# All loads of v on SyncE, and the last rows' products with v behind the odd slot's MLP pieces

## The chip, the cores and the metric

The kernel runs on one core of a Trainium2 chip. The metric is device time in microseconds (us) of one execution, the median of several. Engines are named as in the profile: PE (TensorE matmul), PEld (its weight loads), DVE (VectorE), ACT (ScalarE), POOL (GpSimd), SP (SyncE, which here only issues DMAs). A trailing q (SPq, ACTq) is an engine's sequencer: the row is a DMA issue or a wait, not work of the engine.

## The reference

Attention with a top-32 selection, then an MLP with exact GELU, all in fp32:

```python
scores = scale * np.matmul(q, k.transpose(0, 1, 3, 2))      # (8, 8, 576, 576), head_dim 64
kth = np.partition(scores, -top_k, axis=-1)[..., -top_k:-top_k + 1]
scores = np.where(scores >= kth, scores, -1000000000.0)
...
attn_out = np.matmul(attn, v)                               # softmax of what is left, times v
x = np.ascontiguousarray(attn_out.transpose(0, 2, 1, 3)).reshape(B * S, H * D)   # (4608, 512)
h = x @ w_in                                                # (4608, 2048)
g = 0.5 * h * (1.0 + erf(h * inv_sqrt2))
return (g @ w_out).astype(np.float32)
```

## The kernel before

**Items and slots.** Heads are worked in pairs (4 pairs for each of 8 batches). An item is 128 score rows of a pair: `t` = 0 to 3 are full tiles of 128 rows, and the 64 rows that are left over (`t == NM`, "last rows") are put together from two pairs into one item. There are 144 items, 18 for each batch. Even batches have their two last-row items at the end, odd batches at the start, so four last-row items come in a row: 16 to 19, 52 to 55, 88 to 91 and 124 to 127. The loop over `n` (L1174) is the order of the work, written out by hand. Slot `n` issues the scores of item `n + 2`, the top-32 search of item `n` on DVE (`top_k`, L472), the softmax of item `n - 1` on ACT, the transposition of item `n - 2`, the product with v of item `n - 3` (`attend`, L708), and a number of MLP pieces between them (`mlp`, L1093), each a few matmuls. A slot takes about 10 us.

**Transposing through DRAM.** The product with v needs the softmax matrix transposed (tile `pt`). For a "squared" item (L571) this goes by way of memory: `square_p` (L587) turns 32x32 blocks on DVE (L591), `write_p` (L593) issues four DMAs into a DRAM tile `turned` (L601), and a slot later `read_p` (L603) issues four DMAs that read it back into `pt` (L611). Two items share one `pt` tile, of which there is one, so `read_p` of an even item also waits until the products of the pair of items before it are through. All of these are issued by SP.

**Delayed items.** The last-row items of the three later groups (52 to 55, 88 to 91, 124 to 127) are squared and "delayed" (L577): their products with v (L738, 40 matmuls of 64 columns for an item, 20 for each pair of heads) come a slot later than usual. In the first of the groups: item 52 in slot 56 (L1201), item 53 in slot 57, items 54 and 55 together in slot 59. The list `mid` (L1177) is what is left to do in the odd slots: [53] in slot 57 and [54, 55] in slot 59. Ahead of the MLP pieces of the odd slot (`ODD`, two pieces, then one more, L1242 to L1244) the kernel calls `attend` for the items of `mid`, then the copy to `xT` (`copy_x`, L748 on ACT), then `read_p(n - 3)`. I call the three groups group 1, 2 and 3.

**Loads of v.** There are four buffers of v, one for each pair of a batch. When a buffer has been used for the last time, `attend` issues the load of the next batch's v into it (L753 to L755; `load`, L111): for each of two heads a main part (L134, 128 KB) and a tail of 64 rows (L138, 16 KB). For delayed items the mains go to SP and the tails to ACT's queue: 8 loads for item 52 in slot 56, 8 for item 53 in slot 57, and the same in the other groups, 24 tails in all. In slots whose item `n - 2` is squared, `issue` (L99) holds the loads until `write_p` has been issued (`flush`, L106), so the order on SP at a group is: read of 53, write of 54, loads of v after item 52, read of 54, write of 55, loads of v after item 53, two stores of y, read of 55, write of 56, read of 56. Item 56 is a full tile; its read shares a `pt` tile with item 57, and the product that needs both is L727 in slot 60.

**DMA semaphores.** The DMAs issued by SP and by ACT share eight completion semaphores, given out in turn in the order in which the framework schedules the program. Before a DMA is issued, its queue waits until the DMA that had the same semaphore before it has landed. A DMA on SP can so wait for one that ACT issues.

**PSUM.** The products `o`, the transpositions' `tp_t` and the MLP's product `seven` take turns in one bank (`bank`, L274, tag "z" when `few` is set): each has to wait until ACT has copied out what was there before.

Of the kernel before, what the change touches and what calls it, by code (L numbers as in the profile page):

```python
# [14 lines left out]
def kernel(  # L15
# [19 lines left out]
    nc = tc.nc  # L35
# [10 lines left out]
    NP = H // 2  # L46
# [52 lines left out]
    def issue(f):  # L99

        if held[0]:
            late_issues.append(f)
        else:
            f()
# [472 lines left out]
    def delayed(i):  # L577

        return squared(i) and items[i][1] == NM
# [23 lines left out]
    def read_p(i):  # L603

        if squared(i):
            d = turned.pop(i)
            if i % 2 == 0:
                pt_now[0] = pt_tile()
            cols = slice(i % 2 * P, (i % 2 + 1) * P)
            for k in range(P // SQ):  # L610
                nc.sync.dma_start(  # L611
                    out=pt_now[0][k * SQ : (k + 1) * SQ, :, cols], in_=d[:, :, k, :]
                )
# [77 lines left out]
    def copy_x():  # L691
        while copies:
            copies.pop()()
# [12 lines left out]
    def attend(i):  # L706

        if i < 0 or i >= N:  # L708
            return False
        pair, t = items[i]  # L710
        b, at = divmod(pair, NP)
        if t < NM and t % 2 == 0:
            return False
        pt = pt_now[0]
        both = delayed(i) and i - 1 in starts
        o = shared.pop() if both else bank("o")
        off = 2 * TL if both else 0
        n, row = (2 * P, (t - 1) * P) if t < NM else (TL, SM)
        tok = place_of(b, row)
        gap = RING if t == NM else COLS if tok % RING >= COLS else RING - COLS  # L720
        assert read[0] >= tok - gap + n
        c = slice(column(tok), column(tok) + n)
        if t < NM:
            vt = raw_of("v", pair)
            for j in range(NJ):
                for e in range(2):
                    nc.tensor.matmul(  # L727
                        o[e * D : (e + 1) * D, 0:n], lhsT=vt[:, j, e, :],
                        rhs=pt[:, e * NJ + j if j < NM else NM, :],
                        start=(j == 0), stop=(j == NJ - 1),  # L730
                    )
            copies.append(lambda: nc.scalar.copy(out=xT[:, at, c], in_=o[:, 0:n]))
        else:
            for r in range(2):
                vt = raw_of("v", pair + r)
                for j in range(NJ):
                    for e in range(2):
                        nc.tensor.matmul(  # L738
                            o[e * D : (e + 1) * D, off + r * TL : off + (r + 1) * TL],
                            lhsT=vt[:, j, e, :],  # L740
                            rhs=pt[:, e * NJ + j if j < NM else NM, i % 2 * P :][:, half(r, e)],
                            start=(j == 0), stop=(j == NJ - 1),
                        )
            if delayed(i) and i in starts:
                shared.append(o)
            else:
                first = 0 if both else at
                copies.append(lambda: nc.scalar.copy(  # L748
                    out=xT[:, first : at + 2, c],
                    in_=o[:, 0 : off + 2 * TL].rearrange("p (r n) -> p r n", n=TL),  # L750
                ))

        if t == (NM if b % 2 == 0 else NM - 1):  # L753
            for r in range(2 if t == NM else 1):
                issue(lambda r=r: load("v", pair + r + NP, None, nc.scalar if delayed(i) else None))  # L755
        if at == (NP - 1 if t < NM else NP - 2):
            assert n_tok[0] == tok
            n_tok[0] = tok + n
        return True
# [414 lines left out]
    for n in range(ahead):  # L1174

        held[0] = n < N and squared(n - 2)
        mid = [i for i in (n - 5, n - 4) if delayed(i) and n % 2 and (i % 2 or i in starts)]  # L1177
        if not mid:
            read_p(n - 3)
        left[0] = room_in(n)  # L1180
        few[0] = n > START + 2
        eager[0] = n > N
        left[0] += closes(n - 3) - closes(n - 2)
        if not waits(unit_in(n)):
            weights_add(unit_in(n))
        if n > 0:
            larger(n + 1)
        for piece in squares_in.pop(n, []):
            piece()
        if n == 1:  # L1190

            for e in range(2):
                select(0, e)
            for e in range(2):
                softmax(0, e)
        two = few[0] and n % 2 == 0 and n + 3 < N and items[n + 3][1] < NM
        scores(n + 2, two)
        if two:
            scores(n + 3)
        if delayed(n - 4) and n % 2 == 0 and n - 4 not in starts:  # L1200
            product = attend(n - 4)  # L1201
        else:
            product = not delayed(n - 3) and attend(n - 3)
        late = n > START
        if n != 1 and n < START:

            for e in range(2):
                select(n - 1, e)
            softmax(n - 1, 0)
        copy_x()  # L1210
        if n == START:

            for e in range(2):
                select(n - 1, e)
            softmax(n - 1, 0)
        if waits(unit_in(n)):
            weights_size(unit_in(n))
            weights_add(unit_in(n))
        mlp(1)
        if closes(n - 3):  # L1220
            ready[0] = n_tok[0]
        if few[0] and n % 2:
            run_gelus()
        tr = transposes(n - 2)
        if product and n > START and done[0] < len(pieces) and pieces[done[0]][0] > ready[0]:

            for piece in tr[:1]:
                piece(n + 2 if few[0] else None)
            tr, ready[0] = tr[1:], n_tok[0]
        if not few[0] and n > START:  # L1230
            softmax(n - 1, 0)
        mlp(1)
        if n != 1 and not late:
            softmax(n - 1, 1)
        if few[0]:
            softmax(n - 1, 0)
            if mid:
                for i in mid:
                    attend(i)
                copy_x()  # L1240
                read_p(n - 3)
            if n % 2:  # L1242
                mlp(ODD)
        mlp(1)  # L1244
        prep = prep_in.pop(n, [])
        if n == 0:
            weights_size(unit_in(1))
            keep_busy(14, ident)
        if n == START + 1:

            for piece in prep:
                piece(None)
            prep = []
        if len(prep) > 1 and len(tr) == 3:
            tr, prep = tr[:1] + prep[:1] + tr[1:], prep[1:]
        now = tr[:-1]
        if few[0]:
            now, tr, prep = tr + prep[:1], [], prep[1:]
        for x, piece in enumerate(now):
            piece(n + 2 if few[0] else None)  # L1260
            ready[0] = n_tok[0]
            if few[0] and x == 2:
                break
            mlp(1)
        ready[0] = n_tok[0]
        if late:
            softmax(n - 1, 1)
        if n > 0:
            smaller(n + 1)
        add_small(n - 1)  # L1270
        for piece in tr[-1:] + prep:
            piece(None)
            mlp(1)
        if n < START:

            keep_busy(4 if n == 0 else 8 if product else 14 if n < 5 else 18, ident)

        run_gelus()
        mlp(left[0])
        run_gelus()  # L1280
        if n < N:
            top_k(n, lambda: inverse(n - 1), lambda: square_p(n - 2))
            write_p(n - 2)
            flush()
            if n == 0:
                larger(1)
        else:
            inverse(n - 1)
        threshold(n)
        if n == 0:  # L1290
            smaller(1)
        normalise(n - 1)
        sum_up(n + 2)
        if n in sums_in:
            weight_sums(sums_in[n])
        run_small(6)

        if n > 0 and not waits(unit_in(n + 1)):
            weights_size(unit_in(n + 1))
        run_stores()  # L1300
        if n == N:
            run_stores()
        for m in (n + 1, n + 2):

            if m > 2 and waits(unit_in(m)) == (m == n + 1):
                load_weights(m)
        if n < NP:
            load("v", n)
        if n == 5:
            nc.vector.memset(flat["k"][0][TL:, 0:TL], 0.0)  # L1310
            load("q", SQUARES)
            load("k", SQUARES)
# [38 lines left out]
```

## Time and profile before

| | |
|---|---|
| median of 3 runs | 1493.97 us (1492.85 to 1494.8) |
| the profiled execution: its own time | 1493.65 us |
| its span, first to last instruction | 1491.8 us |
| busy: PE, PEld, DVE, ACT, POOL | 1455.1, 1138.3, 1307.8, 1082.4, 1141.1 us |
| mean granted PE clock | 0.994 |
| DMA packets under 512 bytes | 466464 of 544713 |

A line of a timeline has the start, the time from the start to the end of the last of xN like instructions, engine, source line, operation and tiles; in brackets stands the idle time of the engine just before it and what ended it. A line of the waits has who waited for whom, the total in us, how many times, and the longest. Lines of a source view have durations in ns as least/median/most.

### The profile page before, as it was taken

Reading aid. Unit: us, or ns where it says so; the run is one execution under the profiler, and the core shown is the slowest. Engines: PE = TensorE matmul, PEld = TensorE weight load, DVE = VectorE, ACT = ScalarE, POOL = GpSimd, SP = SyncE. Lnnn points to the kernel's source line nnn. Section 1 sums busy time; section 2 is a strip of 40 time slices with the busy share of each in tenths; the row PEclk is TensorE's granted clock in tenths of the full one; section 3 lists DMA queues with packets and bytes.
Section 4 is the critical chain, followed back from the end, with each engine's and each line's share of the span. In section 5 each row is a group of like instructions: output and inputs, shape, how many; then the busy total and the mean of one; then the engine's idle time right before and its main releaser. Section 6 shows DMA issues by size and latency. Waiting matters only on the chain. (4 is left out here: it accounts for less than half of the span.)

```text
span 1491.8 us, 26509 instructions
## 1 busy us (share of the span) xinstructions
PE 1455.1 (98%) x8693; PEld 1138.3 (76%) x8693; DVE 1307.8 (88%) x3331; ACT 1082.4 (73%) x1899; POOL 1141.1 (76%) x1290
## 2 busy tenths in 40 slices
PE   8999999999999998999999998999999999899999
PEld 6776677887777776877777776787777777687787
DVE  7999899999999997999999999799999999798701
ACT  7999877777777775777777776577777777577630
POOL 6877567877888887877898889687788878787732
PEclk9999999999999999999999999999999999999999
DMA  7425210054444355345534347244543524533300
GB/s 198 141 85 132 74 47 1 23 104 96 88 87 88 59 105 121 64 101 107 101 79 88 70 82 148 57 94 95 100 98 73 102 49 93 121 62 74 71 15 15
DMA packets 544713, 127.04 MB, mean 85 GB/s; under 512 B 466464, under 2 KB 536128, under 8 KB 544576
## 3 DMA queue, kind: packets, MB, share of 16 engines
q1 hardware_dynamic: 541392, 124.54, 39.3%
q8 instruction: 69, 1.13, 0.3%
q10 hardware_dynamic: 3120, 0.79, 0.2%
q14 instruction: 68, 0.56, 0.1%
q0 software_dynamic: 64, 0.03, 0.0%
HBM read 80.47 MB, written 44.83 MB: 84 GB/s over the span
## 5 line engine op out<-in xcount | busy, mean ns | idle before, releaser
L790 PE MATMUL h_ps<-xT,w_in_sb 128*128 128x256 f32 (+1 forms) x2560 | 533.6, 361 | 0.0
L790 PEld LDWEIGHTS h_ps<-xT,w_in_sb 128*128 128x128 f32 x2560 | 437.5, 190 | 74.1 <-issue 25.2
L498 DVE MAX8 top<-lists 128x8 f32<-128x576 f32 (+1 forms) x792 | 475.9, 641 | 0.0
L501 DVE MATCH_REPLACE8 lists<-top,lists 128x288 f32<-128x288 f32 (+1 forms) x528 | 307.9, 589 | 0.0
L567 POOL TENSOR_TENSOR s<-s,stat 128x1152 f32<-128x1152 f32 x135 | 285.8, 2117 | 0.3 <-DVE stat L519 0.3
L532 ACT ACTIVATE s<-s,stat 128x576 f32<-128x576 f32 x288 | 225.0, 790 | 13.0 <-POOL stat L512 12.9
L544 ACT ACTIVATE s<-s,stat 128x576 f32<-128x576 f32 x288 | 225.0, 785 | 11.3 <-POOL lists L462 0.7
L525 POOL TENSOR_SCALAR stat<-stat 128x2 f32<-128x2 f32 x144 | 31.3, 218 | 225.3 <-ACT s L544 211.1
L470 POOL TENSOR_TENSOR lists<-lists 128x576 int32<-128x576 int32 x132 | 186.2, 1411 | 4.0
L462 POOL TENSOR_TENSOR lists<-s 128x576 int32<-128x576 int32 x133 | 187.7, 1412 | 0.0
L806 ACT ACTIVATE g<-h_ps 128x512 f32<-128x512 f32 x144 | 78.2, 594 | 106.0 <-PE h_ps L790 105.7
L727 PE MATMUL o<-pt,raw_v 128*64 128x256 f32 x1280 | 152.9, 384 | 1.9 <-ACT s L544 1.3
L727 PEld LDWEIGHTS o<-pt,raw_v 128*64 128x64 f32 x1280 | 86.8, 136 | 86.7 <-issue 43.2
L946 PE MATMUL y_ps<-w_out_sb,sum 128*128 128x256 f32 x472 | 140.4, 379 | 0.0
L410 ACT ACTIVATE s<-s_ps 128x1024 f32<-128x1024 f32 x127 | 125.3, 1034 | 13.9 <-PE s_ps L402 13.8
L402 PE MATMUL s_ps<-kt,qm 64*128 64x512 f32 x512 | 129.4, 618 | 0.8 <-ACT s L408 0.8
L519 DVE RECIPROCAL stat<-stat 128x2 f32<-128x2 f32 x144 | 23.0, 160 | 109.3 <-POOL stat L525 108.7
L946 PE MATMUL y_ps<-w_out_sb,g 128*128 128x256 f32 x480 | 117.2, 388 | 0.0
L672 ACT COPY pt<-tp 128x1024 f32<-128x1024 f32 x73 | 74.4, 1019 | 56.4 <-PE tp L657 56.3
L501 DVE MATCH_REPLACE8 lists<-first,lists 128x288 f32<-128x288 f32 x264 | 114.3, 439 | 0.0
L498 DVE MAX8 first<-lists 128x8 f32<-128x288 f32 x268 | 106.6, 436 | 0.0
L946 PEld LDWEIGHTS y_ps<-w_out_sb,g 128*128 128x128 f32 x480 | 92.8, 195 | 13.3
(162 smaller groups left out, 2499.7 us busy)
## 6 DMA issues: line engine op xcount, KB each, us to landing
turned<-s SPq DMA_DIRECT2D x240, 144.0 KB, 3.6
pt<-turned SPq DMA_DIRECT2D x240, 144.0 KB, 3.2
raw_v<-in_v_dram SPq DMA_DIRECT2D x64, 128.0 KB, 2.7
raw_q<-in_q_dram SPq DMA_DIRECT2D x112, 72.0 KB, 2.4
raw_k<-in_k_dram SPq DMA_DIRECT2D x112, 72.0 KB, 2.4
out_dram<-y SPq DMA_DIRECT2D x30, 256.0 KB, 2.4
w_out_sb<-in_moe_w_in_dram SPq DMA_DIRECT2D x14, 511.8 KB, 4.8
w_out_sb<-in_moe_w_out_dram SPq DMA_DIRECT2D x10, 511.8 KB, 4.0
```

The source lines that it names most:

```text
L402: nc.tensor.matmul(s_ps[:, e], lhsT=q_t[rows, :], rhs=kt[rows, main_keys(pair)], start=True, stop=True)
L410: nc.scalar.activation(spread(s, S + TL, SM), s_ps, func=AF.Copy, scale=scale)
L462: nc.gpsimd.tensor_tensor(t[:, :, 1].bitcast(i32), a.bitcast(i32), b.bitcast(i32), op=ALU.add)
L470: nc.gpsimd.tensor_tensor(into_of(i)[:, :, 1].bitcast(i32), both, top, op=ALU.subtract)
L498: nc.vector.max(x[:, e], src[:, e])
L501: nc.vector.match_replace(dst[:, e], x[:, e], src[:, e], LOWEST)
L532: nc.scalar.activation(s, s, func=AF.Prelu, bias=st["neg"][:, e : e + 1], scale=1.0, alpha=STEEP)
L544: nc.scalar.activation(s, s, func=AF.Exp, bias=st["bias"][:, e : e + 1], scale=1.0, accum_out=st["den"][:, e : e + 1],)
L567: nc.gpsimd.tensor_tensor(s, s, wide, op=ALU.mult)
L727: nc.tensor.matmul(o[e * D : (e + 1) * D, 0:n], lhsT=vt[:, j, e, :], rhs=pt[:, e * NJ + j if j < NM else NM, :], start=(j == 0), stop=(j = ...
L790: nc.tensor.matmul(h_tile(u)[:, i, :], lhsT=w_in_sb[:, ko, f * P : (f + 1) * P], rhs=xT[:, ko, c0 : c0 + n], start=(ko == 0), stop=(ko == ...
L946: nc.tensor.matmul(acc[names][:, k], lhsT=lhsT, rhs=rhs, start=(j == 0 and k == 0), stop=(j == FT // 2 - 1 and k == 1),)
```

## The change

All loads of v after delayed items are issued by SP, the tails too. In odd slots with two items in `mid` (slots 59, 95 and 131), the `ODD` MLP pieces and one more come ahead of the two items' products, of the copy to `xT` and of the read of item `n - 3`; with one item in `mid` (slots 57, 93 and 129) the order stays.

```diff
@@ -752,7 +752,7 @@
         if t == (NM if b % 2 == 0 else NM - 1):
             for r in range(2 if t == NM else 1):
-                issue(lambda r=r: load("v", pair + r + NP, None, nc.scalar if delayed(i) else None))
+                issue(lambda r=r: load("v", pair + r + NP))
@@ -1177,6 +1177,12 @@
         if not mid:
             read_p(n - 3)
+
+        def mids():
+            for i in mid:
+                attend(i)
+            copy_x()
+            read_p(n - 3)
@@ -1234,13 +1240,13 @@
         if few[0]:
             softmax(n - 1, 0)
-            if mid:
-                for i in mid:
-                    attend(i)
-                copy_x()
-                read_p(n - 3)
+            if len(mid) == 1:
+                mids()
             if n % 2:
                 mlp(ODD)
+            if len(mid) == 2:
+                mlp(1)
+                mids()
         mlp(1)
```

In the built program PE has the same instructions as before; in the three slots six matmuls of y_ps (L946: four with g, two with sums, three pieces) stand ahead of the 80 products (L738) instead of behind them. ACT has 24 DMA issues fewer and SP 24 more, each tail right behind its main; nothing else changes its place.

## The prediction

> **What bounds the kernel now.** I read the engines' busy times first, then who waited for whom, then the timelines of PE and SP around the last rows.
>
> ```profile
> PE 1455.1 (98%) x8693; PEld 1138.3 (76%) x8693; DVE 1307.8 (88%) x3331; ACT 1082.4 (73%) x1899; POOL 1141.1 (76%) x1290
> ...
> PE o L738 <- DMA pt<-turned: 13.7, 3, 4.8
> ...
> SPq L611 <- DMA raw_v<-in_v_dram: 8.5, 4, 3.1
> SPq L134 <- DMA raw_v<-in_v_dram: 8.2, 3, 3.1
> ```
>
> PE works in 98% of the span of 1491.8 us; only 37 us of it are idle, and 13.7 of these are three waits of one kind: a product of last rows waits for its transposed softmax. The two lines of SP say that its queue, which issues that read, stood 16.7 us waiting for loads of v. The change touches both. PE at group 1, one line of slot 57, then slot 59 and the first product of slot 60:
>
> ```profile
> 556.64 1.99 PE L946 MATMUL y_ps<-w_out_sb,g 128*128 128x256 f32 x8
> ...
> 572.43 1.13 PE L944 MATMUL seven<-w_sum,g 128*128 128x256 f32 x4 [0.68 <-POOL g L829]
> 574.02 1.39 PE L738 MATMUL o<-pt,raw_v 128*64 128x64 f32 x40 [0.46 <-ACT p L965]
> 579.56 2.32 PE L738 MATMUL o<-pt,raw_v 128*64 128x64 f32 x40 [4.15 <-DMA pt<-turned]
> 581.81 2.62 PE L946 MATMUL y_ps<-w_out_sb,g 128*128 128x256 f32 x8
> ...
> 585.13 0.38 PE L367 MATMUL tp_t<-kt,qm 128*128 128x128 f32 x2
> ...
> 590.94 2.38 PE L727 MATMUL o<-pt,raw_v 128*64 128x256 f32 x20
> ```
>
> Item 54's product goes at once; item 55's waits 4.15 us. After that wait the clock is low: the same 40 matmuls take 2.32 us instead of 1.39, and the eight behind them 2.62 instead of 1.99. The three MLP pieces (581.81 to 585.13) stand behind the wait, though they need nothing of it. Groups 2 and 3 show the same:
>
> ```profile
> 932.07 2.40 PE L738 MATMUL o<-pt,raw_v 128*64 128x64 f32 x40 [4.78 <-DMA pt<-turned]
> ...
> 944.71 2.38 PE L727 MATMUL o<-pt,raw_v 128*64 128x256 f32 x20
> ...
> 1285.80 2.40 PE L738 MATMUL o<-pt,raw_v 128*64 128x64 f32 x40 [4.75 <-DMA pt<-turned]
> ...
> 1297.38 2.38 PE L727 MATMUL o<-pt,raw_v 128*64 128x256 f32 x20
> ```
>
> SP in group 1: write and read of 53, write of 54, four mains of v, read of 54, write of 55, four mains, two stores, read of 55, write of 56, read of 56:
>
> ```profile
> 541.21 3.73 SPq L601 DMA_DIRECT2D turned<-s  x4
> 547.55 5.03 SPq L611 DMA_DIRECT2D pt<-turned  x4
> 552.72 3.66 SPq L601 DMA_DIRECT2D turned<-s  x4
> 556.48 6.53 SPq L134 DMA_DIRECT2D raw_v<-in_v_dram  x4
> 563.32 2.55 SPq L611 DMA_DIRECT2D pt<-turned  x4
> 566.29 3.51 SPq L601 DMA_DIRECT2D turned<-s  x4
> 569.84 2.95 SPq L134 DMA_DIRECT2D raw_v<-in_v_dram  x4
> 572.90 0.92 SPq L861 DMA_DIRECT2D out_dram<-y  x2
> 573.91 2.56 SPq L611 DMA_DIRECT2D pt<-turned  x4
> 576.59 3.65 SPq L601 DMA_DIRECT2D turned<-s  x4
> 584.35 2.54 SPq L611 DMA_DIRECT2D pt<-turned  x4
> ```
>
> Four reads take 2.55 us to issue, so the second line holds 2.5 us of waiting; four mains take 2.95, so the fourth holds 3.6. By the waits above these are loads of v, and what SP shares its semaphores with there is ACT's tails. From 547 to 579 SP's queue is never done with its work; it, not DVE's transposing, decides when the read of 55 starts (573.91).
>
> **The change, part by part.**
>
> *1. The pieces ahead of the products.* At full clock they are worth 3.3 - 0.6 = 2.7 us, and they have their data: g and its sums are there when "seven" (L944) runs. They start behind it at 573.5, end at 576.2, item 54's product follows, and PE is ready for item 55 at 577.6 instead of 575.4; the 0.46 us for ACT's copy lie beside the pieces. If the read lands when it did, the waits of 4.15, 4.78 and 4.75 us shrink by 2.2 each, and the pieces no longer come behind them.
>
> *2. SP.* Without ACT's tails SP has only its own DMAs to wait for, each for its eighth predecessor, which has landed by the rows above. So I let both waits go. The cost is eight tails a group, four in each of its two sets of loads. Main and tail in turn on SP are seen behind a write of an earlier batch (first and last two of four):
>
> ```profile
> 343.46 0.89 SPq L134 DMA_DIRECT2D raw_v<-in_v_dram  x1
> ...
> 345.48 0.58 SPq L134 DMA_DIRECT2D raw_v<-in_v_dram  x1
> 346.16 0.52 SPq L138 DMA_DIRECT2D raw_v<-in_v_dram  x1
> ```
>
> Two mains and two tails take 3.3 us with the gap behind them (343.46 to 346.75), the next two of each, at the later rate of 1.3 us for one of each, 2.6: a set of eight is 5.9 us against 2.95. Group 1 anew, with DVE's turning of item 54 as the other bound:
>
> ```profile
> 549.07 1.37 DVE L591 STREAM_TRANSPOSE s<-s 128x1152 f32<-128x1152 f32 x1
> ```
>
> Read of 53 issued by 550.1, DVE done at 550.4, write of 54 from 550.5 to 554.0, eight loads to 560.0, read of 54 to 562.7, write of 55 to 566.3, eight loads to 572.2, stores to 573.2, read of 55 from 573.25: 25.7 us after the read of 53, where it was 26.36. In groups 2 and 3 it was 26.0 and 26.3:
>
> ```profile
> 899.32 5.08 SPq L611 DMA_DIRECT2D pt<-turned  x4
> ...
> 925.32 2.59 SPq L611 DMA_DIRECT2D pt<-turned  x4
> ...
> 1253.08 5.56 SPq L611 DMA_DIRECT2D pt<-turned  x4
> ...
> 1279.38 2.57 SPq L611 DMA_DIRECT2D pt<-turned  x4
> ```
>
> So the read of 55 gains 0.65, 0.3 and 0.6 us: 1.5 together. The tails eat most of what the waits give back. Bounds: sets of 5.2 us (2.95 and four tails at 0.55) gain 1.4 us more in each group; a first set in which the 6.53 us were issue and not waiting, with four tails on top (8.8 us), costs 2.9 more.
>
> *3. What is late next.* Slot 60's product (L727) needs the read of 56, and that hangs on SP too. In the source view of that read, group 1, and by its issue in the other two:
>
> ```profile
> DMA to landing us min/median/max: 3.0/3.2/3.5
> ...
> 935.40 2.54 SPq L611 DMA_DIRECT2D pt<-turned  x4
> ...
> 1289.08 2.54 SPq L611 DMA_DIRECT2D pt<-turned  x4
> ```
>
> The last of the four is issued 1.9 us after the first and lands some 3.2 later: 589.5, 940.5 and 1294.2, with the 3.2 us of group 1 taken for all. L727 starts at 590.94, 944.71 and 1297.38: slacks of 1.4, 4.2 and 3.2, **8.8 us together**. PE can gain that, and what the read of 56 itself gains: the 1.5 us of the read of 55, and something because the DMA engines are less pressed:
>
> ```profile
> 572.00:580.00 8.00, 2.96 (x54) 2.40 (x56) 8.00 (x23) 4.17 (x7) 7.26 (x9) 0.98 0.99 233
> ```
>
> DMA (last but one column) is 99% busy there. From the write of 56 to its read takes 7.8 us (576.59 to 584.35); for item 53, with less in flight, 6.3 (541.21 to 547.55). Transfers that now fill the holes left by SP's waits are gone by then: I take half of the 1.4 us in each group, 2.1 together (bounds 0 and 4.2). The sum of this limit: 8.8 + 1.5 + 2.1 = **12.4 us**.
>
> *4. PE without that limit.* It would gain the wait and the low clock behind it: 4.15 + 0.93 + 0.63 = 5.7 us in group 1; 4.78 + 1.01 + 0.63 and 4.75 + 1.01 + 0.63 in the others, 18.5 in all. That is more than 12.4, so part 3 sets the end, and a new wait of about 2 us a group (6.1 over three) is shared between item 55's product and L727.
>
> *5. ACT.*
>
> ```profile
> 552.63 1.28 ACT L806 ACT_TABLE_LOAD   x1 [1.63 <-issue]
> ...
> 555.32 0.86 PE L738 MATMUL o<-pt,raw_v 128*64 128x64 f32 x22 [1.03 <-ACT y L962]
> ```
>
> Issuing the tails keeps ACT until 552.6; its table load, GELU and copy follow, and item 53's product waits 1.03 us for them. What goes of this is between nothing and 1.0 us; I take 0.5, three times 1.5. But PE then only arrives sooner at the wait of part 3, so it adds nothing. That xT's copy and the read of 56 are issued behind the pieces costs nothing either: PE is through with item 55 by 580, and the write of 56 lands after that.
>
> The new waits could lower the clock as the old ones did, at most 0.93 + 0.63 us a group, 4.7. The wait of 1.03 us above is followed by no low clock (the eight matmuls at 556.64 take 1.99), and the new ones are nearer to it: I take nothing. [...]
>
> **The sum.** 1493.65 - 12.4 = 1481.25 for an execution like the profiled one, which lay 0.3 us under the median of 1493.97. Forecast: **1481.5 us**.
>
> **The rivals.**
>
> *PE's limit instead of the read's* (20%). If the read of 56 gains 3.2 us a group (pressure gone, tails cheap), L727 never waits: 18.5 + 1.5 = 20 us, 1473.5 to 1474. For it: DMA at 99% exactly there. Against: SP's sum.
>
> *The tails cost more* (15%). With SP a net 1 to 2 us later in each group, 8.8 - 3 to 6 is left: 1485 to 1491. The clock falling at full price would come to nearly the same (1486).
>
> *Within 0.2%* (5%): SP nearly 3 us later in each group.
>
> *Slower* (8%). SP's waits don't go but move to its own DMAs in flight, and the tails come on top, 5.9 us a group. Then the read of 56 lands 5.9 us later, and L727 starts 4.5, 1.7 and 2.7 us later: 1493.97 + 8.9 = 1503. It decides from 2.9 us (8.8 / 3) a group. For it: full DMA engines hold SP whoever issues. Against: SP's waits end, by the rows, with loads of v that are not in its own queue's order. [...]
>
> **How the numbers follow.** The forecast's case, 1478 to 1485, has 52%. The range, 1473 to 1489, takes in PE's limit and most of the dearer tails; it leaves out same and slower. Faster by over 0.2% (3 us, about what a measurement of this kernel can tell from no change) 0.87, within it 0.05, slower 0.08.
>
> **What would show it.** In the profile after: pieces of L946 ahead of 80 products; waits for the read of 55 of about 1 us a group, and a new one of L727 for pt; SP's waits for raw_v gone, its sets of eight loads at 5.2 to 6 us; 25.7 us from the read of 53 to that of 55. Wrong if L727 doesn't wait (the gain is then near 20), or if SP's sets take over 8 us.

## The result and the profile after

The changed kernel takes **1486.59 us** (median of 5, 1483.89 to 1488.06) against 1492.85 of the kernel before on the same chip: 6.3 us faster, ratio 0.9954 with a 95% interval of 0.9939 to 0.9969. The forecast was 1481.5 in a range of 1473 to 1489. The profiled execution took 1488.04 us with a span of 1486.3, against 1493.65 and 1491.8 before: 5.6 us, 5.5 by the spans, and this is the difference that the traces have to explain.

The waits of PE in the changed kernel: who waited for whom, total, times, longest.

```profile
PE o L738 <- DMA pt<-turned: 5.7, 3, 3.0
PE o L727 <- DMA pt<-turned: 4.4, 2, 2.8
```

The wait for the read of 55 went from 13.7 us to 5.7; a new one of 4.4 stands at slot 60's product. PE's timeline of the change in group 1:

```profile
573.60 1.89 PE L946 MATMUL y_ps<-w_out_sb,g 128*128 128x256 f32 x8
...
576.28 1.39 PE L738 MATMUL o<-pt,raw_v 128*64 128x64 f32 x40
578.90 1.39 PE L738 MATMUL o<-pt,raw_v 128*64 128x64 f32 x40 [1.24 <-DMA pt<-turned]
...
588.95 3.47 PE L727 MATMUL o<-pt,raw_v 128*64 128x256 f32 x20 [2.75 <-DMA pt<-turned]
592.36 3.40 PE L790 MATMUL h_ps<-xT,w_in_sb 128*128 128x256 f32 x12
595.60 0.38 PE L367 MATMUL t_ps<-kt,qm 128*128 128x128 f32 x2
```

The pieces stand ahead of the products, end at 576.2 as forecast, and item 55's product waits 1.24 us instead of 4.15. L727 starts 1.99 us earlier than before (590.94), but behind its wait of 2.75 us the clock is low (0.66 granted from 589.0 to 592.4): its 20 matmuls take 3.47 us instead of 2.38, and the 12 of L790 take 3.40 where the same view of the kernel before has 2.86. Two lines further the gain is 0.34 us:

```profile
593.25 2.86 PE L790 MATMUL h_ps<-xT,w_in_sb 128*128 128x256 f32 x12
595.94 0.38 PE L367 MATMUL t_ps<-kt,qm 128*128 128x128 f32 x2
```

Groups 2 and 3 in PE's timeline of the change:

```profile
932.01 2.40 PE L738 MATMUL o<-pt,raw_v 128*64 128x64 f32 x40 [2.99 <-DMA pt<-turned]
...
942.16 2.38 PE L727 MATMUL o<-pt,raw_v 128*64 128x256 f32 x20
...
1282.09 1.39 PE L738 MATMUL o<-pt,raw_v 128*64 128x64 f32 x40 [1.51 <-DMA pt<-turned]
...
1290.99 2.38 PE L727 MATMUL o<-pt,raw_v 128*64 128x256 f32 x20 [1.61 <-DMA pt<-turned]
```

L727 stands 2.55 and 6.39 us earlier than before, so the groups brought 0.34, 2.2 and 3.8 us. In group 2 the clock is low again behind a wait of 2.99 us, at item 55's product (0.50 granted from 932.0 to 934.4). SP in group 1 of the change (of each set of eight loads the first and the last):

```profile
547.94 2.54 SPq L611 DMA_DIRECT2D pt<-turned  x4
...
554.36 0.78 SPq L134 DMA_DIRECT2D raw_v<-in_v_dram  x1
...
559.66 0.47 SPq L138 DMA_DIRECT2D raw_v<-in_v_dram  x1
560.55 2.78 SPq L611 DMA_DIRECT2D pt<-turned  x4
...
566.85 0.95 SPq L134 DMA_DIRECT2D raw_v<-in_v_dram  x1
...
571.89 0.51 SPq L138 DMA_DIRECT2D raw_v<-in_v_dram  x1
...
573.56 2.59 SPq L611 DMA_DIRECT2D pt<-turned  x4
576.26 3.42 SPq L601 DMA_DIRECT2D turned<-s  x4
583.78 2.54 SPq L611 DMA_DIRECT2D pt<-turned  x4
```

SP's two waits for loads of v, 16.7 us before, are not in its list any more. A set of eight takes 5.8 and 5.6 us here, and the read of 55 starts 25.62 us after the read of 53, where it was 26.36. But the read of 56 still starts 10.22 us after the read of 55 (10.44 before).

One thing lies far from the groups. From group 3's L727 to the end of the span it is 194.4 us before (1491.8 - 1297.38) and 195.3 after. The DMA view of the kernel before, and then of the change, shows the last store, ACT's only one (its last column is the median us from issue to landing), and the queue that carries instructions:

```profile
q14 instruction: 68, 0.56, 0.1%
...
out_dram<-y ACTq DMA_DIRECT2D x1, 128.0 KB, 1.7
```

```profile
q14 instruction: 69, 0.57, 0.1%
...
out_dram<-y ACTq DMA_DIRECT2D x1, 128.0 KB, 2.7
```

It takes 1.0 us longer to land, and the program ends with it.

### The profile page after: what moved, and what is told of

Read it like the earlier page. It is cut to its first block, busy times and chain, and to the rows that moved or that the text cites. A ratio compares the mean times of both kernels' runs of the same rounds, so it can differ in the third digit from the quotient of the medians.

```text
span 1486.3 us, 26513 instructions
## 1 busy us (share of the span) xinstructions
PE 1453.6 (98%) x8693; PEld 1137.4 (77%) x8693; DVE 1307.9 (88%) x3331; ACT 1081.5 (73%) x1899; POOL 1141.0 (77%) x1290
## 5 line engine op out<-in xcount | busy, mean ns | idle before, releaser
L790 PE MATMUL h_ps<-xT,w_in_sb 128*128 128x256 f32 (+1 forms) x2560 | 533.9, 361 | 0.0
L790 PEld LDWEIGHTS h_ps<-xT,w_in_sb 128*128 128x128 f32 x2560 | 438.5, 191 | 73.4 <-issue 25.5
L727 PE MATMUL o<-pt,raw_v 128*64 128x256 f32 x1280 | 154.0, 386 | 6.2 <-DMA pt<-turned 4.4
L727 PEld LDWEIGHTS o<-pt,raw_v 128*64 128x64 f32 x1280 | 87.6, 137 | 91.1 <-issue 44.1
L946 PE MATMUL y_ps<-w_out_sb,sum 128*128 128x256 f32 x472 | 141.1, 381 | 0.0
L946 PE MATMUL y_ps<-w_out_sb,g 128*128 128x256 f32 x480 | 113.7, 380 | 0.0
L437 DVE TENSOR_TENSOR lists<-s 128x576 f32<-128x576 f32 x133 | 101.0, 760 | 0.0
```

Source lines behind the costliest of these rows:

```text
L727: nc.tensor.matmul(o[e * D : (e + 1) * D, 0:n], lhsT=vt[:, j, e, :], rhs=pt[:, e * NJ + j if j < NM else NM, :], start=(j == 0), stop=(j = ...
L790: nc.tensor.matmul(h_tile(u)[:, i, :], lhsT=w_in_sb[:, ko, f * P : (f + 1) * P], rhs=xT[:, ko, c0 : c0 + n], start=(ko == 0), stop=(ko == ...
L946: nc.tensor.matmul(acc[names][:, k], lhsT=lhsT, rhs=rhs, start=(j == 0 and k == 0), stop=(j == FT // 2 - 1 and k == 1),)
```

## The experiments

In all of them the key figure is the time from the start of the read of 53 to that of the read of 56, mean of the three groups: 36.3 us before, 35.7 in the change. Line numbers are shifted by each edit (L739 to L741 of a variant are L738, L728 to L730 are L727). Twelve kernels ran; those whose names begin with the same letter ran on one chip and share its times of the kernel before.

**The two halves.** `e1_order_only` keeps the new order of slots 59, 95 and 131 and gives the tails back to ACT; `e2_loads_only` has the old order and all loads on SP.

```diff
 e1, against the change
-                issue(lambda r=r: load("v", pair + r + NP))
+                issue(lambda r=r: load("v", pair + r + NP, None, nc.scalar if delayed(i) else None))
 e2, against before
-                issue(lambda r=r: load("v", pair + r + NP, None, nc.scalar if delayed(i) else None))
+                issue(lambda r=r: load("v", pair + r + NP))
```

> Pieces ahead of the two products; ACT keeps issuing the tails. Theory (both parts gain, the pieces most of it; waits of over some 2 us are followed by a low clock): the reads of 55 and 56 land as before, the waits for 55 are 2.0, 2.6 and 2.6 us, L727 is held at the slack of 1.4, 4.2 and 3.2 us, and low clocks take up to 1.6 of it in each group: 4 to 7 us faster than before. Rival A (the pieces do it all, the loads nothing): the same as with the whole change, 6 us. Rival B (the loads do it): 0 to 1 us.

> All tails from SP, the pieces behind the products as before. Theory: the read of 55 starts about 0.4 us earlier, ACT's 0.45 us in slot 57 help little, waits of some 3.7 to 4.5 us ahead of item 55's product with low clock behind them stay: 0.5 to 2.5 us faster. Rival A: no difference. Rival B: 5 to 6 us faster. Were the tails' issue all cost, it would be slower.

Measured, with the kernel before at 1495.21 on that chip: e1 1487.36 (ratio 0.9948, 0.9935 to 0.9960), e2 1493.40 (0.9985, 0.9976 to 0.9994). The order alone is worth as much as the whole change, to within the 3 us that the intervals leave; the loads alone bring 2.2 us by the ratio, with an interval of 0.9 to 3.6. Where these 2.2 us lie its profile does not show: its span of 1491.8 us is that of the kernel before on another chip. In e1 SP's waits are back, and with them the wait for the read of 55 is about 3 us (SP's waits, then one line of PE):

```profile
SPq L134 <- DMA raw_v<-in_v_dram: 9.4, 3, 3.2
SPq L611 <- DMA raw_v<-in_v_dram: 8.9, 4, 3.1
```

```profile
580.63 2.40 PE L738 MATMUL o<-pt,raw_v 128*64 128x64 f32 x40 [3.01 <-DMA pt<-turned]
```

Its key figure is 36.9 us, worse than before, and its last store lands in 1.8 us. So in the profiles, what moving the tails gives the reads (1.2 us a group against e1) is mostly lost again at the clock and at the end. The 2 us of e1's theory lie between two rows of the change, 1.61 us of waiting with the clock up behind it and 2.75 with it low; in group 3 of e1 the clock is up behind 2.85 us (40 matmuls in 1.38).

**Which read holds PE.** `e3_stores_later` issues the stores of y behind the read of 55 instead of ahead of it; `e4_keep_clock` adds six matmuls with the identity (12 in the trace, 1.6 us; their result is overwritten) ahead of item 55's product and of L727, so that PE does not idle so long.

```diff
 e3
         if not mid:
             read_p(n - 3)
+            if bare(n):
+                run_stores()
...
-        run_stores()
+        if not bare(n + 1):
+            run_stores()
 e4, in attend
+        if both or (i - 3 in starts and delayed(i - 3)):
+            for _ in range(6):
+                nc.tensor.matmul(o[:, off : off + P], lhsT=ident, rhs=ident, start=True, stop=True)
```

> The whole change, and slot 57's two stores of y are issued by SP behind the read of 55 instead of ahead of it (the same in groups 2 and 3). Theory (SP's order sets when the reads land): the read of 55 starts 1.0 us earlier in each group, the waits for 55 shrink from 1.2, 3.0 and 1.5 to 0.2, 2.0 and 0.5 us; the read of 56 still stands behind the stores on SP and gains nothing by the order alone. 1 to 3 us faster than the change. Rival (the DMA engines' throughput sets the landing): no difference to the change within 1 us.

> The whole change, and 6 matmuls of the identity matrix (1.3 us on PE, their result is overwritten) ahead of item 55's product and of L727 in each group, so that no wait there is over 1.7 us. Theory (the low clock behind the longer waits took some 1.6 us in group 1 and 2 in group 2): the products run at 1.39 and 2.38 us in all groups, 1 to 3 us faster than the change, though the matmuls cost up to 1.3 us where nothing waited. Rival (the clock costs nothing, since the next read holds PE anyway): the same or up to 2 us slower than the change.

Measured on the same chip as e1: e3 1491.16 (0.9971, 0.9961 to 0.9982), a miss, since by the ratios it is 2.5 to 3.4 us slower than the change (f1 below is its second measurement) and not 1 to 3 us faster; e4 1487.36 (0.9943, 0.9930 to 0.9957), by the ratio the same as the change. SP and PE of e3 in group 1:

```profile
572.96 2.58 SPq L611 DMA_DIRECT2D pt<-turned  x4
575.63 1.02 SPq L861 DMA_DIRECT2D out_dram<-y  x2
576.75 5.29 SPq L601 DMA_DIRECT2D turned<-s  x4
584.81 2.54 SPq L611 DMA_DIRECT2D pt<-turned  x4
```

```profile
578.27 1.39 PE L738 MATMUL o<-pt,raw_v 128*64 128x64 f32 x40 [0.73 <-DMA pt<-turned]
...
590.01 4.54 PE L727 MATMUL o<-pt,raw_v 128*64 128x256 f32 x20 [4.44 <-DMA pt<-turned]
```

The read of 55 came 0.6 us earlier and its wait shrank, but the stores and a slower write of 56 (5.29 us of issue instead of 3.42) put the read of 56 a microsecond later: L727 waits 4.44 us, with a low clock behind it (4.54 us for its 20 matmuls). The read of 56 sets the end, not that of 55. In e4 the profile has no low clock (granted clock 1.000 against 0.996), but in groups 1 and 3 PE then waits for the same read, 0.92 and 0.79 us, and in group 2 the added matmuls fill the time.

**SP's queue made shorter, first round.** `f1_change_again` is the change. `f2_stores_behind_write` runs the stores behind the write of 56 (the second hunk of e3 alone). `f3_no_tails` leaves the 24 tails of v out, 64 rows of each head, so its result is another one; PE's work is the same. `f4_stores_and_clock` is f2 with e4's matmuls.

```diff
 f3
-    def load(n, pair, queue=None, queue2=None):
+    def load(n, pair, queue=None, queue2=None, tails=True):
...
-                issue(lambda r=r: load("v", pair + r + NP))
+                issue(lambda r=r: load("v", pair + r + NP, tails=not delayed(i)))
```

> The change as it is, beside the next three. All theories: 5 to 8 us faster than before.

> The change, and the two stores of y are issued behind the write of 56, in which place SP waits for that write's landing anyway. Theory (L727 is held by SP's chain: read of 55, write of 56, its landing, read of 56): all three start 1.0 us earlier in each group, L727 too, and the low clocks of groups 1 and 2 get rarer: 3 to 5 us faster than the change. Rival (the DMA engines' throughput sets the landing, whatever SP's order): within 1 us of the change.

> The change with the 24 tails of v behind delayed items left out (their 64 rows of v stay those of the batch before, so the sums with v are not the reference's; the work of all engines but the DMA queues is the same). Theory: SP's sets cost 3 us instead of 5.6, the reads of 55 and 56 come 3 to 5 us earlier a group and L727 hardly waits: PE's own limit, 10 to 14 us faster than the change (1473 to 1477). Rival (DMA throughput, of which the tails are under a twentieth): at most 2 us faster than the change.

> The stores behind the write of 56 and the 6 matmuls ahead of item 55's product and of L727. Theory: as the stores alone or 1 us faster, since the clock stays up but the waits are short already; with the matmuls costing where nothing waits it may be 1 us slower. A cost of the low clock of 1.6 us a group would show as 2 to 4 us.

Measured, before at 1493.73: f1 1485.98 (0.9948, 0.9934 to 0.9962), f2 1482.93 (0.9931, 0.9919 to 0.9943), f3 1471.88 (0.9856, 0.9842 to 0.9869), f4 1484.26 (0.9938, 0.9926 to 0.9951). Stores behind the write bring about 3 us by the medians; the intervals just overlap, the single executions (1481.86 to 1484.23, and f1's 1484.58 to 1488.29) do not. The key figure falls by only 0.3 us (35.1, f1 35.5), and a part of the 3 us is the clock, 1.000 in f2's profile and 0.997 in f1's; at 1.000 f1 takes 1484.58 and 1485.41, f2 1481.86 to 1482.93. More matmuls on top bring nothing. Without tails 14.1 us more than f1 go, 0.9 of it at the last store (SP, then PE, of f3):

```profile
554.16 3.01 SPq L134 DMA_DIRECT2D raw_v<-in_v_dram  x4
...
564.85 3.01 SPq L134 DMA_DIRECT2D raw_v<-in_v_dram  x4
...
568.97 2.69 SPq L612 DMA_DIRECT2D pt<-turned  x4
...
578.86 2.54 SPq L612 DMA_DIRECT2D pt<-turned  x4
```

```profile
576.27 2.55 PE L739 MATMUL o<-pt,raw_v 128*64 128x64 f32 x80
...
584.68 2.38 PE L728 MATMUL o<-pt,raw_v 128*64 128x256 f32 x20
```

No product waits: this is PE's own limit. The sets of loads take 3.0 us in group 1, and the key figure is 31.1 us. What cost the change its time on SP was the tails, 24 x 16 KB, 0.4 MB of the 127 MB that the program moves. That it is their issue on SP and not their bytes, g1 and h2 show below, where ACT issues them. And even here the read of 56 comes 9.9 to 10.2 us after that of 55.

**The tails elsewhere.** `g1_act_tails_early` is f2, with the tails issued by ACT right behind the copy to xT of their own slot, ahead of its table load (`copies` holds that copy's successors), and not when the held loads are let go. `g2_pool_tails` is f2 with the tails on POOL at the end of the slot.

```diff
 g1
-                issue(lambda r=r: load("v", pair + r + NP))
+                issue(lambda r=r: load("v", pair + r + NP, tails=not delayed(i)))
+                if delayed(i):
+                    copies.insert(0, lambda r=r: load("v", pair + r + NP, None, nc.scalar, mains=False))
 g2, instead of the last two lines, run after sum_up(n + 2)
+                    late_tails.append(lambda r=r: load("v", pair + r + NP, None, nc.gpsimd, mains=False))
```

> Stores behind the write of 56; the tails of v back on ACT, but issued right behind the copy to xT of the item that used the buffer, some 4 us earlier in slots 56 and 57 than before the change, while SP's mains stay behind the write. Theory (tails on SP cost it 2.5 us a set; before the change SP waited for ACT's tails only because they were issued late): the tails have landed when SP comes to their semaphores, SP's sets take 3 us, and the time comes near that without tails: 1472 to 1477 where the change is 1486. Rival (whoever else issues, the eight shared semaphores make the queues wait for each other): ACT's tails now wait for SP's DMAs, and it is 1480 to 1490.

> Stores behind the write of 56; the tails of v issued by POOL at the end of slots 56 and 57, with completion semaphores of their own. Theory: SP as without tails, 1472 to 1477, if POOL's issues (some 0.65 us each, 2.6 in a slot in which POOL is 97% busy) find room; at most 1 to 2 us are lost for these in each of six slots, of which PE sees a part: 1472 to 1482. Rival (POOL sets the slot): slower than the change.

Measured, before at 1493.60: g1 1476.81 (0.9888, 0.9875 to 0.9902), g2 1490.89 (0.9980, 0.9971 to 0.9989). In g2 four issues take POOL 2.14 us, twice in a group, in front of sums that PE needs, and PE's wait for them, 1.0 us in the change, is 5.35. Of the two expectations the rival's came, that POOL sets the slot (POOL, then PE, of g2):

```profile
572.50 2.14 POOL L140 DMA_DIRECT2D raw_v<-in_v_dram  x4
```

```profile
576.94 2.08 PE L948 MATMUL seven<-w_sum,g 128*128 128x256 f32 x4 [5.35 <-POOL g L833]
```

In g1 ACT is through with its first four early, but SP waits for a load of v again in its first set of mains (ACT, then SP, of g1):

```profile
546.28 2.67 ACTq L140 DMA_DIRECT2D raw_v<-in_v_dram  x4
...
556.99 1.85 ACTq L140 DMA_DIRECT2D raw_v<-in_v_dram  x2
```

```profile
554.12 6.84 SPq L135 DMA_DIRECT2D raw_v<-in_v_dram  x4
...
567.41 3.18 SPq L135 DMA_DIRECT2D raw_v<-in_v_dram  x4
```

The first four mains take 6.84 us, of which 3.9 are a wait for a load of v; the second four take 3.18. The load waited for is one of ACT's second set: its first tail goes at 556.99 and lands 2.8 us later, at 559.8, and SP's third main goes at 559.89.

**What of g1 is needed.** `h2_tails_early_alone` is g1 without the moved stores. `h3_first_tails_act` is g1 with only the first set's tails (items 52, 88, 124) on ACT; the second set's go to SP, so that no late issue of ACT's stands between.

```diff
 h3, against g1
-                issue(lambda r=r: load("v", pair + r + NP, tails=not delayed(i)))
-                if delayed(i):
+                issue(lambda r=r: load("v", pair + r + NP, tails=not delayed(i) or i % 2))
+                if delayed(i) and i % 2 == 0:
```

> The change with the tails issued by ACT behind the copy to xT, as before in the early tails, but the two stores stay ahead of the read of 55. Theory (SP's chain to the read of 56 sets the end): the stores cost 1.0 us in each group, so 2 to 4 us slower than early tails and late stores together (1476.8), 1479 to 1481, still 5 us faster than the change. Rival (the early tails do all of it): the same as both together.

> Late stores; only the tails of the first set (behind items 52, 88 and 124) are issued early by ACT, those of the second set by SP behind their mains. Theory: with all tails on ACT, SP's first set still waited 3.9 us for the second set's tails by the shared semaphores; without that wait the first set takes 3.0 us, while the second takes 5.6 instead of 3.2: the read of 56 starts some 1 us earlier a group, and it is 0 to 4 us faster than with all tails on ACT (1473 to 1477). Rival (that wait is covered by the landing of the write of 54 anyway): the second set's 2.4 us are lost, 1478 to 1482.

Measured, before at 1494.23: h2 1479.47 (0.9901, 0.9884 to 0.9918), h3 **1475.36** (0.9875, 0.9861 to 0.9890), the fastest that computes everything; by the intervals it is clearly ahead of the kernel before and of the change, not of g1. h2 lies 2 us above g1 by the ratios, as expected, but the intervals overlap, so beside early tails the stores' place is not shown to matter. SP and PE of h3:

```profile
554.23 4.25 SPq L135 DMA_DIRECT2D raw_v<-in_v_dram  x4
...
570.60 2.66 SPq L613 DMA_DIRECT2D pt<-turned  x4
...
580.98 2.54 SPq L613 DMA_DIRECT2D pt<-turned  x4
```

```profile
576.23 2.55 PE L740 MATMUL o<-pt,raw_v 128*64 128x64 f32 x80
...
586.22 2.38 PE L729 MATMUL o<-pt,raw_v 128*64 128x256 f32 x20 [1.51 <-DMA pt<-turned]
```

The first set takes 4.25 us without a wait for loads of v, the key figure is 33.0 us, no wait for the read of 55 is left, and L727 waits 1.51, 1.04 and 0.82 us.

## Why the prediction was half right

The direction and the mechanism held: PE gains until the read of 56 holds it. The size came out at half, inside the range but outside the forecast's own case of 1478 to 1485, because of three terms of the sum. In the profiled executions:

| term | forecast | in the profile of the change |
|---|---|---|
| slack of L727 | 8.8 | 8.45 |
| read of 55 earlier (SP) | 1.5 | 1.84 (0.74, 0.31, 0.79) |
| read of 56 earlier still (less pressed DMA) | 2.1 | 0.0 (0.22, -0.17, -0.03) |
| low clock behind new waits | 0 | -3.4 |
| last store | not seen | -1.0 |
| read of 53 in group 1 | not seen | -0.4 |
| sum | 12.4 | 5.5, span 5.5 |

**Slack.** Where L727 waits in the change, it starts 5.17 and 5.29 us after the read of 56 starts (588.95 - 583.78, and group 3); I had reckoned 1.9 + 3.2. With 5.25 the slacks of before are 1.3, 4.1 and 3.05. Right.

**SP.** 25.62, 25.69 and 25.51 us from the read of 53 to that of 55, forecast 25.7; sets of 5.8 and 5.6 us in group 1, forecast 5.9. (In f1, the same kernel, the first set of group 1 took 6.75 us and the three stretches are 26.3, 24.8 and 25.2 us, so single sets vary by more than the gain.) That the waits go and the tails eat most of the gain was right, and the slower rival falls with it: no wait of SP for loads of v is left. SP's issue time was most of the matter: f3's key figure is 4.3 us under f1's (35.5), with eight issues less in each group, 0.54 us an issue.

**Pressure: the step that failed first.** I took half of 1.4 us a group because the loads of v would no longer fill the DMA engines behind the write of 56. They do fill them less (DMA share, last but one column; the change, the stretch that stood at 0.99 before):

```profile
572.00:580.00 8.00, 6.13 (x93) 5.34 (x95) 8.00 (x23) 4.05 (x7) 7.26 (x9) 1.00 0.82 203
```

But from the read of 55 to that of 56 it is 10.22, 10.25 and 9.73 us after, 10.44, 10.08 and 9.70 before, and 9.89, 10.12 and 10.15 in f3, which has no tails at all. That stretch is not shortened by fewer loads of v. My own measure, from the write of 56 to its read, did fall, from 7.76, 7.37 and 7.02 us to 7.52, 7.30 and 6.21, half of the 2.1 us; but in groups 2 and 3 the read of 55 ahead of it took 2.83 and 3.41 us to issue instead of 2.59 and 2.57, so the read of 56 gained nothing.

**Clock: the step that cost the profiled execution most.** I took the new waits as too short to lower it, from one wait of 1.03 us, and named 4.7 as the bound. Two of the five did: behind 2.75 us in group 1 (1.09 + 0.54 us lost, at once on the path), and behind 2.99 in group 2, where 1.01 us at item 55's product and 1.9 us of the work behind it make L727 start 7.02 us after its read instead of 5.25, 1.8 us too late. Together 3.4.

The bound was too low as well. I took group 1's 0.63 us for the matmuls behind the wait in all groups; in group 2 of the kernel before they take 3.78 us instead of 1.99, in group 3 2.73:

```profile
934.41 3.78 PE L946 MATMUL y_ps<-w_out_sb,g 128*128 128x256 f32 x8
```

With each group's own rows the three old waits cost 1.6 + 2.8 + 1.8 = 6.1 us by the clock, and PE's limit comes to 19.8 + 1.5 = 21.3 us instead of 20.

The median loses less than the profiled execution. The granted clock of every execution is on record. The profiled one has 0.996, the lowest of the change's five; the two fastest, 1483.89 and 1485.58, have 0.999. In f1 the two at 1.000 take 1484.58 and 1485.41, the profiled one, at 0.997, 1488.29. So f1 gains 8.3 to 9.1 us with the clock up, and 5.4 where it falls as in the profile; what the former lacks to 12.4 is of the size of the pressure and the last store, 3.1. The clock does not explain every execution: one of the change, at 0.998, took 1488.06. And e4, whose clock stays up in all five (0.999 or 1.000), has no better median than the change: its matmuls take the time instead.

**The end.** In the fourteen profiles of this study the last store lands in 2.7 to 2.8 us wherever the instruction queue q14 has 69 packets (the change, f1, e2, e3, e4, f2, f4: those with all tails on SP) and in 1.7 to 1.8 wherever it has 68. That moving 24 issues to SP costs 1 us there is shown by this; that the packet itself is what delays the store is not shown.

**Rivals.** PE's limit, forecast at 20 us, is where f3 stands: 21.9 us, without a wait. For the change it was the wrong bound, as the new wait at L727 said. The measured 1486.6 us falls into the stretch named for dearer tails (1485 to 1491), but the tails cost SP no more than forecast; and it is close to the 1486 named for the clock at full price, which is in part luck, since the clock took 3.4 and not 4.7 even of the profiled execution, and the pressure and the last store make up the rest. e1's equality with the change says more than I had: the order alone gives what the change gives. In the profiles the tails' move to SP gains 1.2 us a group at the reads against e1, 3.7 in all; 0.9 of it goes at the last store, 0.4 at the read of 53 and 1.9 at the clock, where e1 loses 1.5 us by the same reckoning and the change 3.4. The two spans lie 1.1 us apart (1487.4 and 1486.3). By the same sum (8.45, and three times what the key figure gains) h3 should gain 18.4 us and gains 18.9; g1 17.1 and 16.8; h2 15.1 and 14.8; none of these has a low clock in the groups or the late store.

What stays open: when the clock falls behind a wait, since the waits' lengths do not settle it (below), and what makes the last store land later.

## What to carry to other kernels

Moving work ahead of a wait gains only the slack of the next thing that hangs on the same queue (8.45 us here, over three groups); work that slack out first, and from what sets it, here the issue order on SP. Small DMAs are not small on a queue that is never done: count issues, not bytes (0.54 us an issue of 16 KB here), and put them on an engine that can issue them early. Price a new wait on TensorE with a low clock behind it at least as a bound (2.22 us, in f1, was the shortest for a read that had one here; the 20 matmuls behind it lost 0.95), and take the price from each stage's own rows; one row with the clock up behind such a wait, as f2's of 2.78 us, does not rule the fall out.

## What the runs showed of the hardware

**A wait's length does not settle whether the clock falls.** Two lines of PE, the first of f1 in group 2, the second of f2 in group 1:

```profile
941.03 3.33 PE L727 MATMUL o<-pt,raw_v 128*64 128x256 f32 x20 [2.22 <-DMA pt<-turned]
```

```profile
588.45 2.38 PE L727 MATMUL o<-pt,raw_v 128*64 128x256 f32 x20 [2.78 <-DMA pt<-turned]
```

The shorter wait is followed by the low clock (3.33 us for 20 matmuls), the longer one is not. Over the profiles of this study every wait for a read of 2.99 us and more ended low, none of up to 1.8, and between 2.2 and 2.9 both occur. Nor is 1.8 a limit: far ahead of the groups all fourteen profiles have one wait of 1.32 to 1.35 us for POOL. In eleven the four matmuls behind it take 0.44 us, in e2, f4 and h3 0.65 to 0.69, with the low clock (0.84 to 0.86 granted from 70 to 80 us, 1.00 in the others; the line is h3's):

```profile
69.39 0.69 PE L639 MATMUL tp_t<-diag,s 128*64 128x128 f32 x4 [1.33 <-POOL diag L560]
```

So nearly the same wait in the same place is followed by a low clock in one execution and not in another. What else decides it is not shown.

**A queue that waits for another's loads loses by the late ones.** Before, SP stood 16.7 us behind loads of v, and with all tails on its own queue it waits for none; in g1 ACT's first tail goes at 546.3 instead of 550.1, and SP still waits (ACT's issues in the source view of before, with first and last start; SP's waits of g1):

```profile
L138 ACTq DMA_DIRECT2D raw_v<-in_v_dram x24: 472/607/617, 550.1 to 1268.2; - x24
```

```profile
SPq L135 <- DMA raw_v<-in_v_dram: 9.9, 4, 3.9
```

It waits for ACT's second set, as the landing at 559.8 us showed. So it was before: in group 1 ACT issues a tail at 560.74, it lands 1.8 us later, and SP's fourth main goes at 562.64. From issue to landing SP and ACT together have at most eight DMAs in flight, in the trace of before and in that of the change. Yet h2, with the stores where the change has them, is 7 us faster than the change (0.9901 against f1's 0.9948): 24 tails less are issued on SP. In h3 ACT has only the early set, SP's wait is gone but for 0.3 us, and the key figure is 0.4 us lower than g1's, although the second set's tails are back on SP; the two kernels' times are not told apart.
